# Talking-heads attention and feed-forward on one core: 42 score products a batch instead of 48, and output stores issued piece by piece

## The chip, the cores and the metric

The kernel runs on one core of a Trainium2 chip. A core has five engines with a queue each: PE (TensorE, matrix products; its weight loads are listed as PEld), DVE (VectorE), ACT (ScalarE), POOL (GpSimd) and SP (SyncE, which here only issues DMAs). Each works through its queue strictly in order, and they meet at semaphores. The metric is the device time of one execution in microseconds, as the median of several runs. Before the change the three runs took 646.55, 649.42 and 652.16 us.

## The reference

Inputs: q, k, v of (8 batches, 12 heads, 448 rows, 64), two 12x12 mixing matrices, and the weights of a feed-forward layer.

```python
scores = scale * np.matmul(q, k.transpose(0, 1, 3, 2))
scores = np.einsum('bhij,hg->bgij', scores, w_pre)      # mixes the heads
scores = scores - np.max(scores, axis=-1, keepdims=True)
attn = np.exp(scores)
attn = attn / (np.sum(attn, axis=-1, keepdims=True) + 1e-09)
attn = np.einsum('bhij,hg->bgij', attn, w_post)         # mixes them again
out = np.matmul(attn, v)
# heads side by side: x is (3584, 768)
h = np.maximum(x @ w_in, 0.0)                           # (3584, 2048)
return (h * h @ w_out)                                  # (3584, 768)
```

## The kernel before, in words

**Scores.** A matrix product takes a stationary operand of up to 128x128 and streams 448 columns past it. For a pair of heads, `kt` holds both heads' turned k, 64 partitions each (128x448). `qz` holds q turned, with zeros in the other head's 64 partitions, so that a product over all 128 partitions gives one head (L381). The 448 rows of q are split into four blocks of 112 (block r holds rows 4p + r). A batch so needs 12 heads x 4 blocks = 48 score products, each 112x448. Each is evicted from PSUM to `snat` by DVE or ACT (`copy`, L251, so that its records stand at L253 and L255). Two `snat` buffers take turns, one block each.

**Chunks.** Mixing heads needs the heads on partitions. A *chunk* is ten rows of q times twelve heads, 120 partitions. SP moves it from `snat` to a buffer `sch` by one DMA of 120 runs of 448 (a *relayout*, L404); seven `sch` buffers take turns. Then, per chunk: a product with `wmix` mixes the heads (L434), DVE finds the extreme of each row (L439), ACT takes the exponent and its sum (L442), DVE the reciprocal (L448), POOL scales the second mixing matrix by it (L451), four products turn, normalise and mix in one step (L458), and DVE or ACT evicts to `atb` (again L253, L255). A batch has 45 chunks: eleven from each block, and one of eight rows put together from the two rows left over in each block (`schl`, L407). Chunk c of batch b has the number n = 45b + c. After 22 chunks, and after the last, the products with v follow (L503).

**Turning q and k.** In the first two batches TensorE turns them (L301). From the third on, DVE or ACT packs a pair of heads (`pair_k`, `pair_q`) and SP issues two DMA transposes, k at L350 and q at L356. `kt` and `qz` have seven slots for six pairs, so a slot comes free only once the last block of an earlier pair has been scored.

**Feed-forward.** Two batches make 896 rows of x, in four units of 128 or 256 rows. A unit is products with w_in (L547), relu on ACT (L560), squaring on POOL (L563), products with w_out (L579), eviction on DVE (L594), and stores on SP (L622, L629). Since the rows lie in chunk order, a tile of 128 rows is stored in one to five DMAs.

**Order.** All of it is written down ahead of time by a planner (L55). Each operation has an engine or a choice of two, an assumed cost, a due time counted in chunks, and what it depends on. The planner runs through time, gives each free engine the ready operation with the earliest due time, and so fixes the order on every engine. Feed-forward work and stores are due last (FILL, L260) and fill gaps. A relayout is due five chunks ahead of its mix and assumed to take 0.77 us of SP and to land 4.5 us after some 0.4 us more; a DMA transpose takes 1.25 us of SP and lands 6 us later; the stores of one tile are one operation of 1.5 us, however many DMAs they are. On the chip only the order remains, and the semaphores.

Of the kernel before, what the change touches and what calls it, by code (L numbers as in the profile page):

```python
# [10 lines left out]
BF16 = mybir.dt.bfloat16  # L11
# [3 lines left out]
DMODEL = H * D  # L15
# [8 lines left out]
NR = 4  # L24
PR = S // NR
CI = 10
CPR = 11
NP = CI * CPR
KC = CI * H
NCHUNK = NR * CPR + 1  # L30
XA = 2 * NP
# [8 lines left out]
MOST = {"m": 3, "a": 2, "f": 2, "g": 4, "mix": 6}  # L40
UNITS = [(0, 128), (128, 384), (384, 640), (640, 896)]
# [103 lines left out]
def kernel(  # L145
# [20 lines left out]
    qs = sb.tile([PR, H, NR, D], BF16, name="qs")  # L166
    ks = sb.tile([P, H, NB, D], BF16, name="ks")
    vs = sb.tile([P, H, NB, D], BF16, name="vs")
    qz = many(NSLOT, "qz", [P, 2, S], BF16)
    kt = many(NSLOT, "kt", [P, NB * 128], BF16)  # L170
    qn = many(2, "qn", [PR, 2, NR * 128 + 64], BF16)
    kn = many(2, "kn", [P, NB, 2, D], BF16)
    snat = many(2, "snat", [PR, H, S], BF16)
# [16 lines left out]
    def load_q(b, h0, h1, r0=0, r1=NR):  # L190
        nc.gpsimd.dma_start(
            out=qs[:, h0:h1, r0:r1, :].rearrange("p h r d -> p h (r d)"),
            in_=q[b, h0:h1].rearrange("h (p r) d -> p h (r d)", r=NR)[:, :, r0 * D:r1 * D],
        )
# [14 lines left out]
    ident = sb.tile([P, P], BF16, name="ident")  # L209
    for h0 in range(0, H, 4):  # L210
        load_lo(ks, k, 0, h0, h0 + 4)
        load_hi(ks, k, 0, h0, h0 + 4)
        load_q(0, h0, h0 + 4, 0, 1)
        if h0 == 0:
            masks.make_identity(nc, ident[:, :])
    load_q(0, 0, H, 1, NR)
# [6 lines left out]
    for t_ in es:  # L223
# [10 lines left out]
    wmix = sb.tile([KC, P], BF16, name="wmix")  # L234
    nc.vector.memset(wmix[:, KC:P], 0.0)
    wback = sb.tile([KC, H, CI], F32, name="wback")
    nmask = sb.tile([KC, CI], F32, name="nmask")
    nc.gpsimd.tensor_scalar(
        out=nmask[:, :], in0=smask[:, :], scalar1=-SCALE, scalar2=1.0, op0=ALU.mult, op1=ALU.mult,
    )  # L240
    nc.gpsimd.tensor_tensor(
        out=wmix[:, 0:KC].rearrange("p (s h) -> p s h", s=CI),
        in0=wpre_rep[:, :].unsqueeze(1).to_broadcast([KC, CI, H]),
        in1=nmask[:, :].unsqueeze(2).to_broadcast([KC, CI, H]), op=ALU.mult,
    )
    nc.gpsimd.tensor_tensor(
# [39 lines left out]
    def t_qk(b, p):  # L286
# [4 lines left out]
        if i >= NSLOT:  # L291
            old = [score_ops[(i - NSLOT) // NPAIR, NR - 1, 2 * ((i - NSLOT) % NPAIR) + x] for x in range(2)]

        def turn(tag, at, ins, src, n, blocks, dve, act, put):
            key = (tag, "t", b, p, n, blocks[0])

            def mms(slot):
                v_ = slot[:, :].bitcast(BF16)
                for u, r in enumerate(blocks):
                    for x in range(2):  # L300
                        nc.tensor.transpose(  # L301
                            v_[64 * x:64 * x + 64, u * n:(u + 1) * n], src[:, 2 * p + x, r, :], ident[0:n, 0:n],
                        )

            mm = add("PE", 200 + 55 * len(blocks), at, keep(key, mms), ins + old, lat=200, bank=key)
# [6 lines left out]
        def put_q(c0, n):  # L312
            def go(eng, v_):
                for x in range(2):
                    copy(eng, z[64 * x:64 * x + 64, x, c0:c0 + n], v_[64 * x:64 * x + 64, 0:n])
            return go

        first = b == 0
        mk, ek = turn("g", pri, [k_in[b, p // 2]], ks, 128, range(NB), 310, 440, put_k)
        if first:  # L320
            mq, eq = turn("f", pri, [q_in[0, p // 2]], qs, PR, range(1), 300, 520, put_q(0, PR))
            ml, el = turn("g", p - 5, [q_late], qs, PR, range(1, NR), 620, 740, put_q(PR, S - PR))
            ready[b, p] = [[ek, eq]] + [[ek, el]] * 3
            got_op[b, p] = [mk, mq, ml]
        else:
            mq, eq = turn("g", pri, [q_in[b, p // 2]], qs, PR, range(NR), 780, 880, put_q(0, S))
            ready[b, p] = [[ek, eq]] * NR
            got_op[b, p] = [mk, mq]

    ready, got_op = {}, {}  # L330
# [411 lines left out]
```

## Time and profile before

| | |
|---|---|
| runs | 646.55, 649.42, 652.16 us, median 649.42 |
| profiled execution | 649.58 us, span 647.8, mean granted TensorE clock 0.975 |
| TensorE busy | 592.0 us (91%) |
| DVE busy | 509.0 us (79%) |
| ACT busy | 501.9 us (77%) |
| POOL busy | 305.3 us (47%) |
| score products (L381) | 384, 119.4 us busy |
| score evictions | 191 on DVE at 0.614 us, 193 on ACT at 0.544 us |
| relayouts | 352 of 120 runs (0.785 us to issue) and 32 small ones (0.690) |
| DMA transposes | 36 of k (1.217 us to issue) and 36 of q (1.249) |
| stores | 107 (98 at L629, 0.662 us to issue, 9 at L622, 0.461) |

The span runs from the first to the last instruction in the profile; the profiled execution's own time is 1.8 us longer. Busy is the time in which at least one record of the engine runs. In the lists, an entry in square brackets says how long the engine stood idle before the instruction and what ended that wait. SP's DMA issues are not counted as busy, but they stand in the list in order of time with their length. The granted clock is that of TensorE, as a share of full speed.

### The profile page before, as it was taken

The numbers are of one execution on the slowest core, as the hardware profiler recorded it, in microseconds if no ns is written. First come the engines' busy times: TensorE is split into PE (matmuls) and PEld (weight loads), VectorE is DVE, ScalarE is ACT, GpSimd is POOL, SyncE is SP. The second block draws the span as 40 slices with busy tenths as digits, with TensorE's granted clock in tenths as the row PEclk, the third lists the DMA queues.
The fourth block names the chain that finished last, engine by engine and source line by source line (L and its number), as shares of the span: only waits on it lengthen the run. The fifth ranks groups of instructions, "written<-read, shape, count | busy, mean of one in ns | idle before, by whom it ended". The sixth has DMA issues, their size and how long they took to land.

```text
span 647.8 us, 16877 instructions
## 1 busy us (share of the span) xinstructions
PE 592.0 (91%) x5576; PEld 425.1 (66%) x5576; DVE 509.0 (79%) x1274; ACT 501.9 (77%) x1280; POOL 305.3 (47%) x559
## 2 busy tenths in 40 slices
PE   5679799997989999997999989998899989999996
PEld 3347467765667667765767757876666757777874
DVE  7788998995789978984798879997788787988411
ACT  4698799995889878985888868998788868887420
POOL 7245528434635236623556426733464534453531
PEclk9778999998999999999999999999899999999999
DMA  9999949754697549957398567976397845623011
GB/s 106 190 201 185 204 93 192 151 120 117 109 187 141 124 137 167 158 118 117 103 183 141 129 126 143 193 147 118 113 156 155 128 117 131 150 63 109 17 50 49
DMA packets 152500, 86.44 MB, mean 133 GB/s; under 512 B 73757, under 2 KB 148957, under 8 KB 152413
## 3 DMA queue, kind: packets, MB, share of 16 engines
q1 hardware_dynamic: 104253, 62.56, 41.7%
q0 software_dynamic: 48160, 22.81, 27.7%
q8 instruction: 43, 0.70, 0.5%
q14 instruction: 44, 0.36, 0.2%
HBM read 45.62 MB, written 11.01 MB: 87 GB/s over the span
## 4 chain that ended last, share of the span: by engine, by line
PE 62%; DMA 18%; DVE 9%; issue 3%; ACT 3%; POOL 2%; SPq 1%; DVEq 0%; ACTq 0%; POOLq 0%
PE bank L547 16%; PE bank L579 16%; DMA sch<-snat 13%; PE bank L458 9%; PE bank L381 8%; PE bank L434 7%; PE bank L503 6%; DMA qz<-qn 4%; DVE mn L439 3%; ACT es L442 2%; DVE atb L253 2%; DVE snat L253 2%; DMA kt<-kn 2%; POOL wq L451 1%; SPq L404 1%
## 5 line engine op out<-in xcount | busy, mean ns | idle before, releaser
L442 ACT ACTIVATE es<-bank,mn 120x448 bf16<-120x448 f32 x360 | 229.8, 644 | 48.9 <-DVE mn L439 40.3
L451 POOL TENSOR_SCALAR wq<-wback,rc 120x120 bf16<-120x120 f32 x360 | 131.8, 370 | 248.0 <-DVE rc L448 152.5
L439 DVE TENSOR_REDUCE mn<-bank 120x1 f32<-120x448 f32 x360 | 213.8, 613 | 21.0 <-PE bank L434 20.1
L579 PE MATMUL bank<-w,h 128*128 128x384 bf16 x896 | 172.5, 325 | 0.3 <-DVE snat L253 0.3
L547 PE MATMUL bank<-xt,w 128*128 128x256 bf16 (+1 forms) x1536 | 167.3, 262 | 0.0
L253 DVE CAST atb<-bank 128x480 bf16<-128x480 f32 (+1 forms) x214 | 134.4, 637 | 33.3 <-PE bank L458 32.0
L563 POOL TENSOR_TENSOR h<-hr 128x512 bf16<-128x512 f32 x112 | 116.5, 1040 | 72.9 <-ACT hr L560 68.9
L547 PEld LDWEIGHTS <-w 128*128 128x128 bf16 x1536 | 135.0, 98 | 22.3 <-issue 0.8
L434 PE MATMUL bank<-sch,wmix 120*128 120x448 bf16 x352 | 122.0, 365 | 22.3 <-DMA sch<-snat 19.9
L458 PEld LDWEIGHTS <-es 120*128 120x128 bf16 (+1 forms) x1440 | 103.5, 99 | 56.6 <-issue 20.9
L458 PE MATMUL bank<-wq,es 120*128 120x120 bf16 (+1 forms) x1440 | 129.3, 219 | 11.4 <-POOL wq L451 10.2
L253 DVE CAST snat<-bank 112x448 bf16<-112x448 f32 x191 | 114.0, 614 | 18.4 <-PE bank L381 11.9
L381 PE MATMUL bank<-kt,qz 128*112 128x448 bf16 x384 | 119.4, 369 | 8.0 <-DMA qz<-qn 4.1
L579 PEld LDWEIGHTS <-h 128*128 128x128 bf16 x896 | 85.2, 97 | 56.2 <-issue 2.3
L255 ACT CAST snat<-bank 112x448 bf16<-112x448 f32 x193 | 98.4, 544 | 21.6 <-PE bank L381 17.6
L255 ACT CAST atb<-bank 128x480 bf16<-128x480 f32 (+1 forms) x154 | 85.2, 563 | 12.9 <-PE bank L458 11.8
L560 ACT ACTIVATE hr<-bank 128x512 f32<-128x512 f32 x112 | 67.2, 600 | 34.0 <-PE bank L547 32.2
L442 ACT ACTIVATION_READ_ACCUMULATOR es<-bank,mn 120x1 f32 x360 | 75.3, 209 | 0.0
L448 DVE RECIPROCAL rc<-sm 120x1 f32<-120x1 f32 x360 | 54.3, 154 | 21.0 <-ACT es L442 19.2
L381 PEld LDWEIGHTS <-qz 128*112 128x112 bf16 x384 | 48.8, 135 | 24.8 <-DMA qz<-qn 5.5
L434 PEld LDWEIGHTS <-wmix 120*128 120x128 bf16 x360 | 34.8, 100 | 41.4 <-DMA sch<-snat 32.5
L594 DVE COPY osb<-bank 128x384 f32<-128x384 f32 x56 | 30.9, 552 | 34.2 <-PE bank L579 28.0
(41 smaller groups left out, 243.7 us busy)
## 6 DMA issues: line engine op xcount, KB each, us to landing
sch<-snat SPq DMA_DIRECT2D x352, 105.0 KB
qs<-in_q_dram POOLq DMA_DIRECT2D x14, 336.0 KB, 13.5
vs<-in_v_dram POOLq DMA_DIRECT2D x8, 384.0 KB, 7.9
w<-in_moe_w_in_dram POOLq DMA_DIRECT2D x6, 512.0 KB, 11.1
w<-in_moe_w_out_dram POOLq DMA_DIRECT2D x4, 768.0 KB, 15.1
ks<-in_k_dram POOLq DMA_DIRECT2D x14, 192.0 KB, 14.4
out_dram<-osb SPq DMA_DIRECT2D x7, 330.0 KB
vs<-in_v_dram POOLq DMA_DIRECT2D x8, 288.0 KB, 9.6
```

What stands on the lines that cost most here:

```text
L253: nc.vector.tensor_copy(out=out_, in_=in_)
L255: nc.scalar.copy(out=out_, in_=in_)
L381: nc.tensor.matmul(slot[0:PR, 0:S], lhsT=qz[i][:, x, r * PR:(r + 1) * PR], rhs=kt[i][:, 0:S], start=True, stop=True,)
L434: nc.tensor.matmul(slot[:, 0:S], lhsT=wmix[0:rows, :], rhs=src[0:rows, :], start=True, stop=True,)
L439: nc.vector.tensor_reduce(out=mn[i][0:rows, :], in_=slots[mk][0:rows, 0:S], axis=AX.X, op=ALU.min)
L442: nc.scalar.activation(out=es[i][0:rows, 0:S], in_=slots[mk][0:rows, 0:S], func=ACT.Exp, scale=-1.0, bias=mn[i][0:rows, 0:1], accum_out=sm ...
L451: nc.gpsimd.tensor_scalar(out=wq[i][0:rows, :, 0:ns], in0=wback[0:rows, :, 0:ns], scalar1=rc[i][0:rows, 0:1], scalar2=1.0, op0=ALU.mult, o ...
L458: nc.tensor.matmul(slot[:, jb * H * ns:(jb + 1) * H * ns], lhsT=es[i][0:rows, jb * 128:(jb + 1) * 128], rhs=wq[i][0:rows, :, 0:ns], start= ...
L547: nc.tensor.matmul(slot[:, j * w:(j + 1) * w], lhsT=w1[c2][:, (f0 + j) * 128:(f0 + j + 1) * 128], rhs=xt[:, c2, a:z], start=(c2 == 0), sto ...
L560: nc.scalar.activation(out=hr[gi % 2][:, :], in_=slots[key][:, :], func=ACT.Relu)
L563: nc.gpsimd.tensor_tensor(out=h2_[:, f0:f0 + nf, 0:w], in0=hr[gi % 2][:, :].rearrange("p (f c) -> p f c", f=nf), in1=hr[gi % 2][:, :].rear ...
L579: nc.tensor.matmul(slot[:, 0:384], lhsT=h2_[:, ft, mt * 128:(mt + 1) * 128], rhs=w2[:, ft, nt * 384:(nt + 1) * 384], start=(ft == 0), stop ...
```

## The change

The 448 rows of q become three blocks of 128 rows (row 3p + j of the first 384) and a tail of 64 rows for every head. The tails of a pair of heads share one product: `load_tail` reads them into `qt`, row t of head x on partition 2t + x and in that head's 64 columns, with zeros in the others. Turned as a whole (`t_tail` on TensorE in the first two batches, `x_tail` by one DMA transpose a batch after that) it is `zt`, and its product with `kt` gives 64 rows of both heads on 128 partitions. So a batch has 6 + 3 x 12 = 42 score products, each 128x448.

The tail comes first (r = 0) and needs no `qz`. It gives six chunks; its last four rows go, two each, to the thirteenth chunks of blocks 1 and 2, which have eight rows left over; block 3's last chunk has the other eight rows of the 45 chunks' 448. First chunks of the four blocks: 0, 6, 19, 32. As the tails' partitions are ordered by head parity, their mix uses `wmix[0]`, with its rows permuted by one product with `perm` at the start; thirteenth chunks use `wmix[2]`, permuted in part. Buffers `snat` still take turns: block 1 and block 3 share one, the tail and block 2 the other.

In the first batch k and the tails are loaded ahead of the rest of q. The scaling of `wmix` moves from POOL to DVE.

`pieces` replaces `store`: each DMA of a tile's store is an operation of its own, of 0.45 us up to ten rows and 0.85 us above.

The diff, cut:

```diff
-NR = 4
-PR = S // NR
+NJ = 3
 CI = 10
-CPR = 11
-NP = CI * CPR
+CPR = 12
+NS = 64
+TAIL = S - NS
 KC = CI * H
-NCHUNK = NR * CPR + 1
-XA = 2 * NP
+C0 = [0, 6, 19, 32]
+NCHUNK = 45
+XA = 22 * CI
 XB = S - XA
 NB = 4
 W2B = 2 * S
...
+SEGS = [(0, 0, 60, TAIL)]
+for j_ in range(NJ):
+    SEGS.append((2, 60 + 130 * j_, 120, j_))
+    SEGS.append((1, 180 + 130 * j_, 8, j_))
+    if j_ < NJ - 1:
+        SEGS.append((0, 188 + 130 * j_, 2, TAIL + 60 + 2 * j_))
...
-    qs = sb.tile([PR, H, NR, D], BF16, name="qs")
+    qs = sb.tile([P, H, NJ, D], BF16, name="qs")
+    qt = sb.tile([P, NPAIR, P], BF16, name="qt")
+    zt = sb.tile([P, NPAIR, P], BF16, name="zt")
...
-    qz = many(NSLOT, "qz", [P, 2, S], BF16)
+    qz = many(NSLOT, "qz", [P, 2, NJ * P], BF16)
...
-    snat = many(2, "snat", [PR, H, S], BF16)
+    snat = many(2, "snat", [P, H, S], BF16)
...
+    for t_ in wmix[1:]:
+        nc.vector.tensor_tensor(
...
+        def put_q(eng, v_):
+            for x in range(2):
+                copy(eng, z[64 * x:64 * x + 64, x, :], v_[64 * x:64 * x + 64, 0:NJ * P])
+
+        mk, ek = turn("g", pri, [k_in[b, p // 2]], ks, NB, 310, 440, put_k)
+        at = p - 5 if b == 0 else pri + 3
+        mq, eq = turn("g", at, [q_in[b, p // 2]], qs, NJ, 700, 800, put_q)
+        ready[b, p] = [[ek]] + [[ek, eq]] * NJ
+        got_op[b, p] = [mk, mq]
...
+        pri = b * NCHUNK - 19 + 3 * g
+        mm = add("PE", 200, pri, keep(key, mms), [tail_in[b]] + old, lat=200, bank=key)
+        ev = add({"DVE": 360, "ACT": 440}, 0, pri, put, [mm], frees=key)
...
+    def x_tail(b):
+        old = [score_ops[b - 1, 0, p] for p in range(NPAIR)]
+
+        def turn():
+            nc.sync.dma_start(
+                out=zt[:, :, :], in_=qt[:, :, :].rearrange("p a c -> p (a c)"), transpose=True,
+            )
+
+        pri = b * NCHUNK - 22
+        op = add("SP", 1250, pri, turn, [tail_in[b]] + old)
+        done = add("TURN", 800, pri, lambda: None, [op], lat=6000)
+        got_tail[b] = [done]
+        for p in range(NPAIR):
+            ready_tail[b, p] = done
+
...
-        ready[b, p] = [[tk_op[i], tq_op[i]]] * NR
+        ready[b, p] = [[tk_op[i]]] + [[tk_op[i], tq_op[i]]] * NJ
...
     def score(b, r, h):
-        p, x = divmod(h, 2)
+        p, x = (h, 0) if r == 0 else divmod(h, 2)
...
-        sn = snat[(b * NR + r) % 2]
-        tag = "mfag"[h % 4] if b == 0 and r == 0 else "g"
+        sn = snat[(b * (NJ + 1) + r) % 2]
...
         def mms(slot):
-            nc.tensor.matmul(
-                slot[0:PR, 0:S], lhsT=qz[i][:, x, r * PR:(r + 1) * PR], rhs=kt[i][:, 0:S], start=True, stop=True,
-            )
+            w = zt[:, p, :] if r == 0 else qz[i][:, x, (r - 1) * P:r * P]
+            nc.tensor.matmul(slot[:, 0:S], lhsT=w, rhs=kt[i][:, 0:S], start=True, stop=True)
 
         def evac(eng):
-            copy(eng, sn[:, h, :], slots[key][0:PR, 0:S])
-
-        pri = b * NCHUNK + CPR * r - AHEAD - 9 + 0.7 * h
-        n = b * NR + r - 2
+            copy(eng, sn[:, h, :], slots[key][:, 0:S])
+
+        nh = NPAIR if r == 0 else H
+        pri = b * NCHUNK + C0[r] - AHEAD - 0.6 - 0.7 * (nh - h)
+        n = b * (NJ + 1) + r - 2
         old = list(relay_of[n]) if n >= 0 else []
-        mm = add("PE", 190, pri, keep(key, mms), ready[b, p][r] + old, lat=200, bank=key)
...
+        sn = snat[(b * (NJ + 1) + r) % 2]
+        lat = 5500 if b == 0 and c else 4500
+        here = relay_of.setdefault(b * (NJ + 1) + r, [])
+        deps = [scopy[b, r, h] for h in range(NPAIR if r == 0 else H)]
+        pri = n - AHEAD
+        if r > 0 and cc == CPR and r < NJ:
+            src_of[n] = schl[r - 1]
+            here.append(move(n, pri, 700, deps + side.get((b - 1, r), []), schl[r - 1][0:96, :], sn[120:P, :, :], lat))
+            return
+        src_of[n] = sch[len(ring) % NSCH]
+        old = [m_op[ring[-NSCH]]] if len(ring) >= NSCH else []
+        ring.append(n)
+        if r == 0:
+            srcs, rows = sn[2 * CI * cc:2 * CI * (cc + 1), 0:NPAIR, :], KC
+        elif cc == CPR:
+            srcs, rows = sn[120:P, :, :], 96
+        else:
+            srcs, rows = sn[cc:cc + CPR * (CI - 1) + 1:CPR, :, :], KC
+        here.append(move(n, pri, 770, deps + old, src_of[n][0:rows, :], srcs, lat))
+        if r == 0 and cc == 5:
+            for j in range(1, NJ):
+                here.append(move(
+                    b * NCHUNK + C0[j + 1] - 1, pri + 0.5, 500, deps + side.get((b - 1, j), []),
+                    schl[j - 1][96:KC, :], sn[116 + 4 * j:120 + 4 * j, 0:NPAIR, :], lat,
+                ))
...
+        wm = wmix[0 if r == 0 else 2 if cc == CPR else 1]
...
+        half = 0 if c < 22 else 1
+        m = m_op[n] = add("PE", 190, n, keep(mk, f_m), relay[n] + [at_op.get(n - NE), w_ready], lat=200, bank=mk)
...
-                if z == W2B and mt == 1 and pair == B // 2 - 1:
-                    add("SP", 1500, FILL, lambda si=si, mt=mt, nt=nt: store(pair, a + mt * 128, osb[si % 2], nt), [ev])
...
-            ix_store[0] += 1
-            sp = add("SP", 1500, FILL, lambda si=si, mt=mt: store(pair, a + mt * 128, osb[si % 2]), [ev0, ev])
-            st_op[si] = add("DMA", 800, FILL, lambda: None, [sp], lat=2500)
+                whole = not (z == W2B and mt == 1 and pair == B // 2 - 1)
+                evs = evs + [ev] if nt == 1 and whole else [ev]
+                if nt == 1 or not whole:
+                    done = []
+                    for rows, dst, o in pieces(pair, a + mt * 128, None if whole else nt):
+                        def store(dst=dst, o=o, rows=rows, si=si, e0=0 if whole else nt * 384, e1=384 if not whole and nt == 0 else DMODEL):
+                            nc.sync.dma_start(out=dst, in_=osb[si % 2][o:o + rows, e0:e1])
+                        done.append(add("SP", 450 if rows <= CI else 850, FILL, store, evs))
+                    st_op[si] = add("DMA", 800, FILL, lambda: None, done, lat=2500)
...
+    def w_turn(slot):
+        nc.tensor.matmul(
+            slot[0:KC, 0:KC], lhsT=perm[:, :], rhs=wmix[1][:, 0:KC], start=True, stop=True,
+        )
...
+        if b < 2:
+            t_tail(b, 0)
+            t_tail(b, 1)
+        else:
+            x_tail(b)
...
+                    if g0 == 0:
+                        tails = [load(1e5, n, lambda b=b, x=x: load_tail(b + 1, x), got_tail[b] + gate(n)) for x in range(2)]
+                        tail_in[b + 1] = add("DMA", 0, n, lambda: None, tails, lat=0)
```

## The prediction

> **What bounds the kernel now.** I read the page first: the share of each engine, the forty slices, the chain that ended last.
>
> ```profile
> span 647.8 us, 16877 instructions
> PE 592.0 (91%) x5576; PEld 425.1 (66%) x5576; DVE 509.0 (79%) x1274; ACT 501.9 (77%) x1280; POOL 305.3 (47%) x559
> ...
> PE   5679799997989999997999989998899989999996
> ...
> PEclk9778999998999999999999999999899999999999
> ...
> PE 62%; DMA 18%; DVE 9%; issue 3%; ACT 3%; POOL 2%; SPq 1%; DVEq 0%; ACTq 0%; POOLq 0%
> ```
>
> TensorE is full except at the start, at the end and in a few dips of one or two slices. The 592 us overstate its work, since a matmul's record holds its drain: the list in order of time shows products of 448 columns starting 0.19 us apart, though each record is 0.35 us long. So one 448-column product costs 0.19 us where TensorE is full.
>
> The dips come about once in 75 us, where one batch hands over to the next. The windows, the list in order of time and the waits show what ends them:
>
> ```profile
> 296.00:300.00 4.00, 4.00 (x42) 3.43 (x39) 2.38 (x6) 3.56 (x10) 2.66 (x5) 1.00 0.77 120
> 300.00:304.00 4.00, 0.94 (x8) 0.53 (x7) 0.58 (x2) 0.82 (x2) 1.86 (x3) 1.00 1.24 105
> 304.00:308.00 4.00, 3.43 (x16) 2.00 (x16) 1.48 (x4) 1.63 (x4) 0.46 (x1) 0.59 0.78 137
> ```
> ```profile
> 303.15 0.58 PE L381 MATMUL bank<-kt,qz 128*112 128x448 bf16 x2 [3.02 <-DMA qz<-qn]
> ```
> ```profile
> 449.39 0.80 SPq L629 DMA_DIRECT2D out_dram<-osb  x1
> 450.30 1.25 SPq L356 DMA_TRANSPOSE qz<-qn  x1
> 451.64 3.71 SPq L404 DMA_DIRECT2D sch<-snat  x4
> ```
> ```profile
> 454.82 0.50 PE L434 MATMUL bank<-sch,wmix 120*128 120x448 bf16 x1 [3.43 <-DMA sch<-snat]
> ```
> ```profile
> PE bank L434 <- DMA sch<-snat: 19.9, 26, 3.4
> ```
>
> In the windows the columns after the length are the busy times of PE, PEld, DVE, ACT and POOL, then the granted clock. At 300 us TensorE stands 3.0 us for a turned q and then runs 4 us at a clock of 0.59. At 451 us a relayout is issued late, behind a store and a q turn on SP, and its mixing product comes 3.43 us late; at 154 us it is the same (3.00 us). From 80 to 600 us the 40 us windows add up to 28 us without TensorE, 16.5 us of it (40 to 600 us) in front of mixing products that wait for a relayout.
>
> **The change, part by part**, against the profiled execution (649.58 us, span 647.8, 1.8 us around it; the median of the runs, 649.42, is the same to 0.03%). The compiled order of the changed program gives the counts.
>
> *Score products:* 384 become 336. That the change does not do this is excluded, the order has 336. 48 x 0.19 = 9.1 us of TensorE. In the first two batches, where TensorE turns q, 96 transposes become 72 and 13 come in (12 of tails, one for the mixing matrix): 11 fewer, at 24 in 0.78 us (16.65 us) 0.4 us. Beside full TensorE both count: **-9.5**. If the stretch is bound otherwise the gain there is nothing: bounds 0 and -9.5; I take all, because in 240 to 280 us TensorE lacks only 0.55 of 40 us.
>
> *Evictions:* 48 fewer, at 0.614 us on DVE and 0.544 us on ACT: 27.8 us, 14 on each. That those of 128 partitions take as long as those of 112 I take from the eviction of 128x456, 0.546 us on ACT. The copies of q (`pair_q`, L343) shrink from 512 to 384 columns: 36 x a quarter of 0.28 to 0.64 us, 4 us in all. This lies beside TensorE, save where the chain runs through evictions; it gives them 2% (DVE snat) and not much more on ACT, some 16 us, an eighth of which goes: **-2** (bounds 0 and -16, the 14 and 2 of each engine, were these the limit).
>
> *q off the first block:* tails need k and zt; q is needed only by block 1. The answer on tile qz:
>
> ```profile
> its engine sat idle before it (us, times) until:
>   DMA qz<-qn: 9.6, 9
> ```
>
> zt is turned at 24 to 29 chunks ahead of its batch, some 40 us, so it is no wait. But the last turn of k is issued 2 to 5 chunks ahead, and the last product of the first block stands 2 to 5 chunks ahead of the batch (3 to 5 before): one SP issue earlier than the last q, no more. So I take half of the 9.6, the clock's dips with it: **-5**. Bounds 0 and -14 (9.6, and 4.3 for the three slow stretches: 5 us at 0.70, 4 at 0.71, 4 at 0.59).
>
> *SP:* relayouts 384 -> 376 (8 more large, 16 fewer small: 8 x 0.79 - 16 x 0.69 = -4.7), six turns of qt at 1.25 (+7.5; a narrower q turn costs what a k turn does, 1.22 to 1.25), stores 107 -> 126 (79 small instead of 47 at 0.46, 47 large instead of 60 at 0.82: +4.1). Sum +6.9 us in 648, about 1 us a batch on a queue that issues about 61 us a batch (44 x 0.79, 4 x 0.69, 12 x 1.25, 13.4 stores of 0.63) of 75. Against that, a store of several pieces was planned as one piece of 1.5 us whatever its length (four took 2.66 us at 307.92), and each piece now has its own place and a cost near the measured one: a relayout is held up by one piece, at most 0.86 us. Behind each turn and piece on SP stand relayouts, and behind those the mixing product. **0**, bounds -8 (half of the 16.5) and +7.
>
> *The new wait:* block 1's twelve products can only be planned once block 3 of the batch before has left its buffer (both are snat1), and all stand within two chunks, 8 to 6 chunks ahead of the first mix that needs them. The planner assumes 4.5 us for a relayout's landing; the first one here landed after 6.5 us (15.88 to 22.41). Their evictions wait for it at the head of DVE and ACT, with the minima, exponents and atb copies behind them, and TensorE's next mixes behind those. Nearest row: evictions waiting for sch, 3.9 us in 7 and 2.2 in 2, 0.7 us each. Seven batches at 0.7: **+5**. Bounds 0 and 7 x 3.4 (the longest wait for a relayout) = +24.
>
> *Start and end:* the first relayout needs 6 evictions and no q copies instead of 12 and 12 (3 to 3.5 us less on each of two engines), but DVE's prelude grows by a 0.38 us memset and four or five small operations of about 0.25 us, and block 1, needed six chunks later instead of eleven, still waits for the same q loads. **-1**, bounds -3 and +2. The last store goes from three issues to two, 0.4 us, inside that. POOL has 14 more load issues at 0.7 to 0.8 us beside 47% busy: 0. The tails' loads have the 64-element runs of the first q loads (3.8 us to land) and come in the previous batch: 0.
>
> Sum: -9.5 - 2 - 5 + 0 + 5 - 1 = -12.5: 649.6 becomes **637**.
>
> [...]
>
> **The rivals.**
>
> *Slower: the turnover of block 1 stalls.* The burst of twelve evictions meets a late relayout in each of seven batches; DVE and ACT stand, block 1's first relayouts are issued late on an SP that is already full there (125.99 to 155 us shows it issuing without a pause), and TensorE runs out of filler. Price: 7 x (3.4 us of wait + 1.5 us at the low clock, the mean of the three dips' 4.3) = 34, less 9.5 + 2 + 1: +21, **671**; it decides from about 2 us a batch lost (14 of the 17.5 that the other terms gain). For it: the dips of today are of this kind, on the same queue. Against: the last products of a block stood 6 chunks ahead of use before too, and evictions waited little. [...]
>
> *No change: the gain is eaten.* TensorE has less work but stands for the same relayouts, and the new wait takes 7 x 1.0: -9.5 + 7 - 1 = **646**. For it: 16.5 us of idle come from relayouts, which the change does not shorten.
>
> [...]
>
> **How the numbers follow.** Forecast 637, its own range 629 to 643: 0.48. No change, around 646: 0.20. Faster still: 0.15. Slower: 0.17. The runs of before spread from 646.55 to 652.16, so 1% is about what can be told from no change; below 642.9 lies the forecast nearly whole and the fast rival: faster 0.63, within 1% 0.21, slower 0.16. The range 621 to 655 leaves out most of the slow rival and the edge of the fast one.
>
> **What would show it.** 336 score products still 0.19 us apart, and TensorE's busy time down by 9 to 15 us (0.31 us of record a product at most). Idle before score products on qz near 0. The three clock dips at the even batches gone or shorter; the wait of mixing products for sch no longer than 20 us. Evictions waiting for sch under 10 us in all: more than 20 is the slow rival. SP's busy time up by about 7 us. I am wrong if TensorE's busy time falls and its idle time grows as much, or if block 1's first mix, seven times, stands more than 2 us.

## The result and the profile after

The changed kernel takes 672.1 us (median; 668.8 to 674.9) against 648.9 of the kernel before on the same chips: ratio **1.035**, 95% interval 1.028 to 1.042. It is 3.5% slower where 637 us, 1.9% faster, was forecast. The profiled execution took 671.08 us. Of `mem_own_pe`, below, three runs of ten took 654 to 659 us and are not counted.

First the page of the changed kernel:

```profile
span 669.1 us, 16736 instructions
PE 595.3 (89%) x5517; PEld 419.3 (63%) x5517; DVE 501.3 (75%) x1258; ACT 488.9 (73%) x1241; POOL 313.9 (47%) x572
...
PE   5768799986879989798889998989997998999997
...
PEclk9668799998999999799989998999999998999999
...
PE 64%; DMA 20%; DVE 8%; issue 3%; SPq 2%; POOL 1%; ACT 1%; DVEq 0%; ACTq 0%; POOLq 0%
```

TensorE's busy time has not fallen (592.0 before), and there are more dips than before, in the middle of batches too. The waits of TensorE and of SP's queue (engine, line, what it waited for: us in total, times, longest) say for what:

```profile
PE bank L504 <- DMA sch<-snat: 35.9, 28, 5.0
...
PE bank L436 <- DVE snat L277: 6.3, 4, 3.1
PE bank L436 <- DMA kt<-kn: 4.9, 6, 1.6
```
```profile
SPq L372 <- DMA qt<-in_q_dram: 26.0, 6, 6.7
```

L504 is now the mixing product, L436 the score product, L372 the turn of the tails. No score product waits for a turned q on its way (`DMA qz<-qn`) any more; the wait of mixing products for relayouts rose from 19.9 to 35.9 us; and SP, which issues every relayout, stands 26.0 us in front of six turns until the tails have landed. The third such turn, in the lists in order of time of POOL, SP and TensorE:

```profile
253.90 0.90 POOL L200 DMA_DIRECT2D qs<-in_q_dram  x1
254.80 0.67 POOL L211 DMA_DIRECT2D ks<-in_k_dram  x1
255.45 0.68 POOL L217 DMA_DIRECT2D ks<-in_k_dram  x1
256.10 1.37 POOL L206 DMA_DIRECT2D qt<-in_q_dram  x2
```
```profile
261.45 0.62 SPq L665 DMA_DIRECT2D out_dram<-osb  x1
267.72 1.26 SPq L372 DMA_TRANSPOSE zt<-qt  x1
269.08 6.68 SPq L459 DMA_DIRECT2D sch<-snat  x7
```
```profile
275.95 0.56 PE L504 MATMUL bank<-sch,wmix 120*128 120x448 bf16 x1 [4.96 <-DMA sch<-snat]
```
```profile
264.00:272.00 8.00, 7.00 (x68) 5.55 (x66) 7.21 (x19) 6.96 (x20) 6.76 (x11) 1.00 1.34 167
272.00:280.00 8.00, 4.05 (x15) 2.18 (x16) 2.47 (x5) 2.60 (x7) 2.36 (x5) 0.65 0.97 198
```

The tails' load is issued behind one of q and two of k. SP issues nothing from 262.1 to 267.7. Seven relayouts follow at 269, too late: TensorE stands 4.96 us, and the clock is 0.65 in the window of 272 to 280. The DMA packets in the trace show a second delay behind the first. Packets of SP's queue that start in each us (a relayout moves packets of 896 bytes, the turn of 256):

```
us from the start    267  268  269  270  271  272  273  274  275
relayouts (896 B)     39    7    0    0    0    0   24  113  103
the turn (256 B)       0    0  273   65   93  324   13    0    0
```

This turn's own transfer takes 4.15 us beside the loads, and until it is through no packet of a relayout starts.

Where the 21.3 us of span come from can be read from the spans. *Idle* is the span less TensorE's busy time. *Clock* is (1 - mean clock) x span: what the lowered clock adds to the busy time, a little too much, since part of it is idle. Busy less clock is TensorE's work at full clock. In the changed kernel products of 448 columns start 0.37 us apart at a clock of 0.5 and 0.19 at 1.0 (medians of L504 and L436). Each row is one profiled execution; that of `pe_lumped` was the shortest of its kernel's runs, those of `pe_turn` and `before_minus48_order` the longest of theirs.

| profiled execution | span | idle | clock | work |
|---|---|---|---|---|
| before | 647.8 | 55.8 | 16.2 | 575.8 |
| after | 669.1 | 73.8 | 32.1 | 563.2 |
| `turn_late` | 649.7 | 64.1 | 23.4 | 562.2 |
| `pe_tail` | 647.8 | 60.8 | 24.0 | 563.0 |
| `pe_wait` | 655.1 | 68.1 | 24.9 | 562.1 |
| `pe_turn` | 666.4 | 72.4 | 34.7 | 559.3 |
| `pe_lumped` | 640.9 | 56.0 | 22.4 | 562.5 |
| `before_minus48_order` | 654.3 | 67.1 | 20.3 | 566.9 |

The work fell by 12.6 us, somewhat more than the 9.5 forecast; idle rose by 18.0 and the clock's part by 15.9.

### The profile page after: what moved, and what is told of

Read it like the earlier page. It is cut to its first block, busy times and chain, and to the rows that moved or that the text cites. A ratio compares the mean times of both kernels' runs of the same rounds, so it can differ in the third digit from the quotient of the medians.

```text
span 669.1 us, 16736 instructions
## 1 busy us (share of the span) xinstructions
PE 595.3 (89%) x5517; PEld 419.3 (63%) x5517; DVE 501.3 (75%) x1258; ACT 488.9 (73%) x1241; POOL 313.9 (47%) x572
## 4 chain that ended last, share of the span: by engine, by line
PE 64%; DMA 20%; DVE 8%; issue 3%; SPq 2%; POOL 1%; ACT 1%; DVEq 0%; ACTq 0%; POOLq 0%
PE bank L641 18%; PE bank L609 16%; DMA sch<-snat 14%; PE bank L528 8%; PE bank L504 8%; PE bank L436 7%; PE bank L565 6%; DVE mn L509 3%; DMA kt<-kn 2%; DVE atb L277 2%; DMA qt<-in_q_dram 2%; DVE snat L277 1%; DMA schl<-snat 1%; SPq L459 1%; DVE rc L518 1%
## 5 line engine op out<-in xcount | busy, mean ns | idle before, releaser
L521 POOL TENSOR_SCALAR wq<-wback,rc 120x120 bf16<-120x120 f32 x360 | 130.1, 366 | 254.2 <-DVE rc L518 149.8
L509 DVE TENSOR_REDUCE mn<-bank 120x1 f32<-120x448 f32 x360 | 213.8, 613 | 23.4 <-PE bank L504 22.2
L277 DVE CAST atb<-bank 128x480 bf16<-128x480 f32 (+1 forms) x224 | 143.7, 650 | 54.6 <-PE bank L528 52.2
L641 PE MATMUL bank<-w,h 128*128 128x384 bf16 x896 | 176.7, 330 | 0.7 <-DVE snat L277 0.4
L504 PE MATMUL bank<-sch,wmix 120*128 120x448 bf16 (+1 forms) x344 | 120.4, 370 | 38.2 <-DMA sch<-snat 35.9
L609 PEld LDWEIGHTS <-w 128*128 128x128 bf16 x1536 | 137.2, 100 | 24.5 <-issue 0.4
L279 ACT CAST snat<-bank 128x448 bf16<-128x448 f32 x175 | 89.0, 544 | 34.7 <-PE bank L436 28.2
L277 DVE CAST snat<-bank 128x448 bf16<-128x448 f32 x161 | 96.2, 615 | 22.1 <-PE bank L436 11.7
L436 PE MATMUL bank<-kt,qz 128*128 128x448 bf16 x288 | 89.1, 374 | 7.6 <-DVE snat L277 6.3
L279 ACT CAST atb<-bank 128x480 bf16<-128x480 f32 (+1 forms) x136 | 77.5, 573 | 18.9 <-PE bank L528 18.1
L504 PEld LDWEIGHTS <-wmix 120*128 120x128 bf16 x360 | 35.1, 100 | 52.9 <-DMA sch<-snat 40.0
L436 PEld LDWEIGHTS <-qz 128*128 128x128 bf16 x288 | 28.6, 103 | 30.8 <-issue 16.2
```

What stands on the lines that cost most here:

```text
L277: nc.vector.tensor_copy(out=out_, in_=in_)
L279: nc.scalar.copy(out=out_, in_=in_)
L436: nc.tensor.matmul(slot[:, 0:S], lhsT=w, rhs=kt[i][:, 0:S], start=True, stop=True)
L504: nc.tensor.matmul(slot[:, 0:S], lhsT=wm[0:rows, :], rhs=src[0:rows, :], start=True, stop=True,)
L509: nc.vector.tensor_reduce(out=mn[i][0:rows, :], in_=slots[mk][0:rows, 0:S], axis=AX.X, op=ALU.min)
L521: nc.gpsimd.tensor_scalar(out=wq[i][0:rows, :, 0:ns], in0=wback[0:rows, :, 0:ns], scalar1=rc[i][0:rows, 0:1], scalar2=1.0, op0=ALU.mult, o ...
```

## The experiments

One thing holds for nearly all of them. Whenever an edit changes what the planner plans, it writes another order for PE, DVE, ACT and POOL as well: the traces show their instructions in another sequence. Only `before_minus48_order`, `before_noloads` and `pe_lumped_noloads` keep the sequence of PE, DVE and ACT of the kernel that they start from. What a new order does without any other change was measured three times: -1.5 us (`before_1400`), +8.6 us (`before_pieces`) and +8.4 us (`before_minus48` against `before_minus48_order`). So a difference of up to some 9 us between two of the other kernels is not by itself the price of the edit.

### Is it the turn of the tails?

Four kernels. `turn_late` issues the turn later:

```diff
         def turn():
+            with tc.issue_after(relay_ins[b * NCHUNK - 20].ins):
                 nc.sync.dma_start(out=zt..., in_=qt..., transpose=True)
...
-        op = add("SP", 1250, pri, turn, [tail_in[b]] + old)
+        op = add("SP", 1250, pri, turn, [tail_in[b], relay[b * NCHUNK - 20][0]] + old)
```

> The changed kernel with one difference: SyncE may issue the turn of the tails (zt) only behind the relayout that runs 20 chunks ahead of the batch, so it stands 17 to 18 chunks before its batch instead of 24 to 29; nothing else moves. Theory 1 (the queue of SyncE stands in front of this turn for the tails' load, 26.0 us in six batches, the relayouts behind it come late, and TensorE waits for them and then runs at a lower clock): the 26 us go to under 5, the mixing products' wait for relayed chunks falls from 35.9 us to 15 to 22, and the time is 650 to 658. Theory 2 (the turnover of snat before block 1, the prediction's slow rival, makes the loss): no change, 668 to 674. Theory 3 (the stores, now 450 to 850 us in pieces on the planner's account, displace relayouts): no change, 668 to 674.

`pe_tail` has no such turn:

```diff
-        if b < 2:
-            t_tail(b, 0)
-            t_tail(b, 1)
-        else:
-            x_tail(b)
+        t_tail(b, 0)
+        t_tail(b, 1)
```

> The changed kernel with the tails turned on TensorE, as in the first two batches, in all eight: six transposes and two evictions of 384 columns a batch more, one turn on SyncE and its wait less in batches 2 to 7. Theory 1: SyncE no longer waits for a load ahead of a batch; the evictions cost 6 x 0.8 = 5 us of VectorE and ScalarE and the transposes 6 x 0.4 = 2 us of TensorE; 650 to 660. Theories 2 and 3: 672 to 680, since only work is added.

`before_plus_turn` adds `load_tail` (for one pair of heads) and `x_tail`, both unused, to the kernel before.

> The kernel before, with, added and unused, a small load of tails into a tile qt (64 rows of one pair of heads, two transfers a batch) behind its loads of q and k, and one turn of this tile on SyncE in batches 2 to 7; nothing else. It prices the turn's place in SyncE's order apart from the blocks. Theory 1: SyncE stands in front of the added turn for some 20 to 30 us in all, and the kernel gets slower by 6 to 20 us: 655 to 669. Theories 2 and 3: at most the turns' own issue, 6 x 1.25 us, partly hidden: 647 to 653.

`load_first` moves the two lines that load the tails ahead of `got`, the loads of q and k.

> The changed kernel with the two loads of the tails issued ahead of the loads of q and k on GpSimd's queue, in place of behind them; the turn stays where SyncE's order has it, 28 to 31 chunks ahead. Theory 1 (SyncE waits for the tails' load, which is issued late and lands slowly): the 26 us of SyncE's wait fall below 8, and the time is 648 to 658. If the turn itself, or the count of its packets, were the price: 668 to 674.

Measured: `turn_late` **650.9** (ratio to before 1.005, 1.001 to 1.009), `pe_tail` **648.1** (0.998, 0.995 to 1.002), `before_plus_turn` **667.3** (1.029, 1.023 to 1.034), `load_first` **669.7** (1.029, 1.025 to 1.033). So the turn, at the place that it has on SP, is worth 21 to 24 us, more than an order alone did; the blocks of 128 rows without it are as fast as the kernel before, and the kernel before with such a turn, of one pair of heads, is 18 us slower. SP's wait in `before_plus_turn`:

```profile
SPq L344 <- DMA qt<-in_q_dram: 28.5, 6, 7.5
```

`turn_late` met its time but not the whole of its account. SP's wait for the tails is gone and "nothing else moves" does not hold, since the order is new; the wait of mixing products stayed above the expected 15 to 22 us. It and that of `pe_tail`:

```profile
PE bank L508 <- DMA sch<-snat: 29.2, 27, 3.2
```
```profile
PE bank L504 <- DMA sch<-snat: 23.6, 20, 3.0
```

`load_first` was a miss for the wait as the only cause:

```profile
SPq L372 <- DMA qt<-in_q_dram: 11.9, 7, 3.4
```

The wait fell from 26.0 us to this, though not below 8, and the time hardly moved. The turn then stood 28 to 31 chunks ahead, amid the loads. So wait and transfer were separated. Both kernels are `pe_tail` with one DMA a batch added on SP, 24 to 28 chunks ahead:

```diff
 # pe_wait
+            nc.sync.dma_start(out=scr[0:1, :], in_=qt[0:1, 0, 0:D])
 # pe_turn
+            with tc.issue_after(relay_ins[b * NCHUNK - 29].ins):
+                nc.sync.dma_start(out=scr[:, :, :], in_=w2[:, 0, 0:5 * P], transpose=True)
```

> The changed kernel with the tails turned on TensorE (648.1), and, added in batches 2 to 7, a copy of 128 bytes on SyncE that waits for the tails' load and stands 24 to 28 chunks ahead of the batch, where the changed kernel has its turn. It brings back the wait without the turn's transfer. If the wait in SyncE's order is the cause: SyncE waits some 25 us for the load and the time is 664 to 674. If the turn's own transfer beside the loads is the cause: 646 to 652.

> The same as the run above with the other half: in the same places of SyncE's order a turn of 128 x 640 elements that waits for no load (its source is a weight that has long landed; the result is unused). If the wait is the cause: 647 to 654, the turns' issue of 6 x 1.3 us at most. If the transfer beside the loads is the cause, as the run with the loads issued first (669.7) suggests: 662 to 674.

Measured: `pe_wait` **657.3** (1.013, 1.008 to 1.018), `pe_turn` **663.4** (1.020, 1.014 to 1.027), against 648.1 of `pe_tail`. The kernel with the wait alone is 9 us slower, that with the transfer alone 15. `pe_wait` so lies between its two expectations, `pe_turn` in that of the transfer. In `pe_wait`:

```profile
SPq L373 <- DMA qt<-in_q_dram: 24.4, 6, 7.7
```
```profile
PE bank L501 <- DMA sch<-snat: 33.2, 22, 5.8
```

and in `pe_turn`, where SP waits for no tail:

```profile
PE bank L504 <- DMA sch<-snat: 42.6, 31, 4.3
```

against the 23.6 us of `pe_tail`. In both it is mixing products that stand without their relayout, but not at the same chunks. The six turns of the changed kernel are issued in batches 1 to 6, between the twelfth and the eighteenth mix of the batch. The starts of the mixing products give the time from mix 8 to mix 20, added up over these six batches:

| | mix 8 to mix 20, six batches |
|---|---|
| before | 108.2 us |
| after | 132.4 |
| `turn_late` | 112.2 |
| `pe_tail` | 110.8 |
| `before_plus_turn` | 125.1 |
| `load_first` | 133.0 |
| `pe_wait` | 124.7 |
| `pe_turn` | 115.6 |

The changed kernel loses 24 us to the kernel before in these stretches, as much as its whole loss, and `pe_tail` loses 3. So the loss stands where the turn stands, whatever the new order does elsewhere. The wait alone is seen at work in the same way: `pe_wait` takes 14 us more than `pe_tail` here, some of which it wins back elsewhere. The transfer is not: `pe_turn` loses 5 us of its 15 here, and three of its four longest waits for a relayout (4.3, 3.1 and 2.6 us) stand at chunks 39 to 43 of a batch, over twenty chunks behind the turn. So the wait is shown; that the transfer alone costs 15 us is not, since a new order could account for the rest.

### Is it the stores in pieces?

`before_pieces` is the kernel before with the change's `pieces`; `after_lumped` and `pe_lumped` undo it in the changed kernel and in `pe_tail`:

```diff
-                    for rows, dst, o in pieces(...):
-                        def store(...): nc.sync.dma_start(...)
-                        done.append(add("SP", 450 if rows <= CI else 850, FILL, store, evs))
+                    def store(...):
+                        for rows, dst, o in pieces(...): nc.sync.dma_start(...)
+                    done = [add("SP", 1500, FILL, store, evs)]
```

> The kernel before with its stores as one operation of the plan for each piece (450 or 850 ns) in place of 1500 ns for a tile; the same DMAs. Theory 3 (piecewise stores push relayouts back): slower by 5 us or more, 654 to 665. Theories 1 and 2: within 1%, 645 to 654; the prediction had 0 for this part.

> The changed kernel with its stores planned as before, one operation of 1500 ns for all pieces of a tile; the DMAs are the same. In the kernel before, the split of this operation cost 8.6 us (657.7 against 649.1). If that price is the same in the changed kernel: 661 to 666 against 672. If it is a matter of where the planner happens to put things in the old kernel, or if the late relayouts hide it: 669 to 675.

> The changed kernel with both: the tails turned on TensorE in all batches (648.1 by itself) and the stores planned as one operation a tile. If the stores' split costs what it cost in the kernel before: 637 to 642. If it costs nothing here: 645 to 651.

`before_1400` replaces 1500 by 1400 in the kernel before.

> The kernel before with one number of the plan changed: a tile's store counts 1400 ns in place of 1500; the instructions and their DMAs are the same, only the order that the planner writes moves. It measures what such a reordering alone does to the time. If the +8.6 us of the stores in pieces was the price of the pieces: within 2 us of the kernel before, 647 to 651. If orders of the planner scatter by some us whatever the reason: any time from 643 to 660, and differences of a few us between such variants say nothing of the edit.

Measured: `before_pieces` **657.7** (1.015, 1.010 to 1.019), `after_lumped` **666.1** (1.027, 1.021 to 1.033), `pe_lumped` **645.2** (0.992, 0.989 to 0.995), `before_1400` **648.4** (0.998, 0.997 to 1.000). The pieces cost 8.6 us in the kernel before; in the changed one the medians differ by 6.0 (with intervals that overlap), in `pe_tail` by 2.9 (intervals that just overlap). The DMAs of each pair are the same, so this is the order alone; that a new order need not cost anything, `before_1400` shows. Why the finer account gives a worse order was not found out.

`pe_lumped` ran once more under the label `pe_lumped_1400` (the number in it means nothing):

> The kernel with the tails turned on TensorE and one planned store a tile (645.2) once more, on another chip and in five rounds, beside the three above. If its gain is real: 642 to 648 and an interval below 1.

It took **643.9** (0.993, 0.990 to 0.996). Tails on TensorE and one planned store a tile make the change a version that is 0.7 to 0.8% faster than the kernel before. Whether these 4 to 5 us come from the blocks of 128 rows or from this version's order is not shown.

### Is it the new wait of block 1?

`mem_own_pe` gives the tails' products a buffer of their own, in space that `mem_pe` frees too:

```diff
-        sn = snat[(b * (NJ + 1) + r) % 2]
+        sn = stail if r == 0 else snat[(b * NJ + r - 1) % 2]
```

> A control for the next: the changed kernel with the tails turned on TensorE, and with space freed in SBUF: six buffers of qz in place of eight, hr and wback in bf16, the permutation kept in a tile of weights that is overwritten later. hr in bf16 halves what the hidden layer's eviction writes and what its following step on GpSimd reads, which may gain some us; six buffers of qz bind the turn of q to the batch before. Within 1% of 648: 642 to 654 by all theories.

> The control with, in the freed space, a buffer of its own for the products of the tails, so that blocks 1 to 3 alternate over the two snat buffers and block 1 no longer waits for the relayouts of the last block of the batch before; its products stand 19 to 7 chunks ahead and no longer in a burst 8 to 6 chunks ahead. Theory 2 in its small form (the prediction's +5 for this turnover): 4 to 10 us below the control, 638 to 644 if the control is at 648. Theory 2 in its large form (the slow rival, 34 us): 20 us or more below it. If the turnover costs nothing: within 2 us of the control.

Measured: `mem_pe` **647.9** (0.999, 0.996 to 1.001) and `mem_own_pe` **651.0** (1.001, 0.997 to 1.005; seven runs from 643 to 652). Taking the wait away gains nothing that can be seen. In `mem_pe` score products wait 7.8 us for evictions or relayouts; in `mem_own_pe` these waits are gone, but the mixing products' wait rose from 22.1 to 30.2 us. The two versions also differ in their order, and a gain of a few us may hide behind that. The large form, 20 us or more, is excluded.

### Where does the gain on the products stay?

Two kernels leave 48 products and their evictions out of the kernel before; in `before_minus48` `score` returns early for the odd heads of block 3, in `before_minus48_order` the planner still plans them:

```diff
         def mms(slot):
+            if r == NR - 1 and h % 2:
+                return
...
         def evac(eng):
+            if r < NR - 1 or h % 2 == 0:
                 copy(eng, sn[:, h, :], slots[key][0:PR, 0:S])
```

> The kernel before with 48 score products and their 48 evictions left out (the odd heads of the fourth block of each batch are not computed; the old values are relayed in their place), nothing else changed. It prices the saving of the change apart from all that the change adds. If a product pays its 0.19 us of TensorE, as in the prediction: 9 us and, with the evictions' bounds, up to 16 less, 633 to 641. If the products fill time that TensorE would spend waiting or at a lower clock: 645 to 650.

> The kernel before without the 48 products and 48 evictions of the odd heads of the fourth block, as in the earlier run (661.2), but the planner still plans them, so that every other instruction stays in the order of the kernel before. If the earlier run was slow because the planner wrote another order: 636 to 644 here, the products' 9 to 12 us being gained. If less work on TensorE only lets it run into the relayouts earlier and stand there, whatever the order: 646 to 664.

Measured: **661.2** (1.019, 1.016 to 1.022) and **652.8** (1.006, 1.003 to 1.009). Leaving work out made the kernel slower, by 11 us with a new order and by 4 us in the old one. The old order's waits of TensorE:

```profile
PE bank L437 <- DMA sch<-snat: 24.6, 26, 2.6
...
PE bank L383 <- DMA qz<-qn: 5.1, 4, 3.3
```

against 19.9 and 4.1 before. In the table above its work is 8.9 us less than before, its idle time 11.3 more, its clock's part 4.1 more, in an execution that is 3 us above the median. The work left out came back as idle time and a lower clock. Of the idle time, 4.7 us more stands in front of mixing products and 1.0 in front of products that wait for q; that TensorE, with less to do, only reaches the relayouts earlier is the likely reading, but these rows carry half of it at most.

Three kernels leave out loads, to see whether this happens in the loads' bursts. `pe_lumped_noload` drops the tails' loads from the second batch on, from the plan too (`tails = []`); in the other two `lambda: load_q(...)` becomes `lambda: b < 1 and load_q(...)`, and so for k, v and the tails, and the planner still plans them:

> The changed kernel with the tails turned on TensorE and the stores planned as one operation a tile (645.2), and, from the second batch on, without the loads of the tails (the first batch's tails are used again): 7 x 2 transfers of 384 packets of 128 bytes fewer. If these packets cost time beside the other transfers: 638 to 643. If not: 643 to 648.

> The kernel before without its 48 loads of q, k and v for the third to the eighth batch (old values are used again); every other instruction stays in its order. With the next run it tells whether the loads' burst, in which relayouts land late, is what holds the kernel back. If it does: 625 to 640. If the loads cost nothing: 646 to 651.

> The repaired version of the change (tails turned on TensorE, one planned store a tile; 644 to 645) without the loads of q, k, v and the tails for the third to the eighth batch. If the gain on the products, 9 to 12 us of TensorE's work, is eaten in the loads' bursts alone: 8 to 12 us below the run above. If it is eaten by waits and a lowered clock anywhere, the bursts or not: the same 4 to 6 us below it as with the loads.

Measured: `pe_lumped_noload` **642.0** (0.989, 0.986 to 0.993), `before_noloads` **639.5** (0.984, 0.982 to 0.987), `pe_lumped_noloads` **636.5** (0.981, 0.978 to 0.983). The loads cost 10 us in the kernel before and 7 to 9 in the repaired change. Without the tails' loads it is 2 to 3 us faster, in a new order, so that this is not shown to be the price of their packets. Without loads the repaired change is ahead of the kernel before by 3.0 us, with them by 4 to 5. So the 9 to 13 us of work are not lost in the bursts; most of them turn into waits and low clock elsewhere too. That it is the pace of the relayouts which decides there is an argument: what a faster pace would give was not tried.

## Why the prediction was wrong

**The turn of the tails: this step failed.** The prediction wrote "zt is turned at 24 to 29 chunks ahead of its batch, some 40 us, so it is no wait", "the tails' loads ... come in the previous batch: 0" and, for SP, six turns of 1.25 us of issue. All three ask whether the *user* of zt waits, and it never does. None asks what stands in SP's queue *behind* the turn, an operation that waits for a load that POOL issues last: the next relayouts, which are issued 7.2 us (median) ahead of their mixes. SP's issue time, the sum of its DMA issues' lengths, was forecast well (468.1 to 478.2 us, +10 where +7 was said); the 26.0 us of waiting and the six transfers, 2.1 to 5.8 us each, were not in the term, which was 0 with +7 as its upper bound. The runs give 24 us for it (672.1 less 648.1), the whole of the loss of 23, and the stretch from mix 8 to mix 20 gives the same 24. How much of it is the wait and how much the transfer stays open: with the wait alone a kernel is 9 us slower, with a small turn and the wait 18, and the 15 us of the transfer alone lie for the most part elsewhere.

**The order.** The section on the kernel before says that the planner "fixes the order on every engine". That is wrong for SP: the set handed to `manual_schedule` at the kernel's end names PE, DVE, ACT and POOL. SP's own order is left to the framework, and the turn stands in it 24 to 29 chunks ahead where the planner's due time is 22. "Each piece now has its own place" on SP therefore did not follow from the planner's costs: the pieces changed what the planner believed of SP, and through that the order of the other four, which is another one in the trace of `before_pieces`. The term was part of the same 0; it measured +3 to +9.

**Score products, -9.5.** The count and the size are right: 336 products, work down by 12.6 us. What failed is taking all of it off the time "because in 240 to 280 us TensorE lacks only 0.55 of 40". One full window stood for a span with 55.8 us of idle time, and the lower bound of 0 that the prediction itself named was the better value: in the kernel before, in its own order, leaving out 48 products made the time 0.6% longer.

**Evictions, -2.** DVE and ACT lost 7.7 and 13.0 us of busy time, 20.7 in all. Neither is the bound; no run shows a gain from it.

**q off the first block, -5.** The wait for turned q is gone, as said. In its place score products wait 4.9 us for kt ("the last turn of k is issued 2 to 5 chunks ahead") and 6.3 us for evictions. So no gain is left of it, and none shows in any version.

**The new wait, +5.** No run shows it: `mem_own_pe` has it not and is not faster. Evictions waited for relayouts once, 4.6 us on DVE, where over 20 us was the mark of the slow rival.

**The slow rival** gave 671 us and the kernel took 672. That was luck: as the cause of the loss its mechanism is refuted. Taking block 1's turnover away did not help, taking the turn away gave all back, and the four waits of over 1 us behind a turn (2.7, 5.0, 1.1 and 4.4 us) stand at chunks 15 to 17 of a batch, not at its end, where that turnover is. The waits at the end of a batch are no worse than before (1.1 to 2.9 us at chunks 40 to 43 after, 1.0 to 3.4 before). A time that fits is no evidence for the mechanism behind it.

**The fast rival** did not come either: no score product waits for a turned q any more and the stores are planned piece by piece, but the clock's part of the span grew from 16.2 to 32.1 us.

**Start, -1.** The first mix came at 21.26 us instead of 22.41. Not foreseen was the handover from the first batch to the second: at the sixteenth mix of batch 1 the changed kernel is 3.8 us behind the kernel before and `pe_tail` 5.6, with a clock of 0.83 and 0.84 in place of 1.00 in the window of 60 to 80 us. Its cause was not tested.

**The marks for being wrong.** The first, TensorE's busy time falling while idle grows as much, came in a harsher form: work fell by 12.6 us and idle grew by 18.0, but the lowered clock stretched the records (a score product's from 0.35 us at 1.0 to 0.58 at 0.5), so that busy time did not fall at all (592.0 to 595.3 us, where 9 to 15 less was forecast). The second, block 1's first mix standing more than 2 us, did not come: that mix waits for nothing in any of the eight batches.

## What to carry to other kernels

When a DMA that waits for something is put into a queue that others share, ask first what stands behind it in that queue, and only then whether its user waits. Ask the same of its transfer: at the third turn no packet of a relayout started for 4.15 us, until the turn was through, though what that costs alone was not settled here. Time saved on the busiest engine counts only where that engine's work, and not a chain that feeds it, sets the pace: take the engine's idle time over the whole span as the measure, and leave the work out once, in the same order, to see what it is worth. A planner's costs steer only the queues that it is given, and any change to them can rewrite the order of all the others: compare the time of the stretch in which the edit acts, and not the total alone.

## What the runs showed of the hardware

*A wait of 2.03 us was followed by a lower clock, one of 2.04 us was not.* In `pe_tail` one wait of 2.03 us, with no other beside it, stands ahead of a stretch at half the clock:

```profile
384.46 0.35 PE L504 MATMUL bank<-sch,wmix 120*128 120x448 bf16 x1 [2.03 <-DMA sch<-snat]
```
```profile
380.00:382.00 2.00, 2.00 (x37) 1.91 (x35) 0.99 (x4) 2.00 (x7) 0.78 (x3) 1.00 0.43 84
382.00:384.00 2.00, 0.43 (x6) 0.18 (x4) 1.25 (x3) 0.72 (x3) 2.00 (x3) 1.00 0.64 211
384.00:386.00 2.00, 1.54 (x10) 0.86 (x10) 0.00 (x0) 0.57 (x1) 0.29 (x1) 0.75 0.51 96
386.00:388.00 2.00, 2.00 (x22) 2.00 (x20) 1.15 (x2) 1.19 (x3) 0.00 (x0) 0.50 0.59 182
388.00:390.00 2.00, 2.00 (x18) 1.35 (x17) 1.21 (x5) 1.74 (x5) 0.65 (x1) 0.90 0.46 135
```

The clock (the eighth figure, after POOL's) is 0.50 in the window of 386 to 388, with TensorE full before and after the wait. A wait of 2.04 us in the changed kernel is followed by no such stretch; its clock stays at 1.00 until 346 us:

```profile
322.40 0.36 PE L504 MATMUL bank<-sch,wmix 120*128 120x448 bf16 x1 [2.04 <-DMA sch<-snat]
```

The clock records tell the two apart. In the traces of the kernels before and after, every change between 1.0 and 0.5 falls on a grid of 3.413 us in each, to within 2 ns. Taking the windows of that grid from 100 us on, up to the last with a whole one behind it, by TensorE's busy share in them: of the 311 at full clock ten are busy for 1% to 40%, and each is followed by a window at 0.5; of the 301 others, the lowest busy for 47% and 48%, none is. Of the windows at 0.5 the ten that are busy for 83% or more are followed by full clock, and the two that are busy for 54% and 78% by another at 0.5. So there half the clock, for 3.4 us or longer, followed each time where TensorE stood for 2.06 us or more in all within one window (60% of 3.413), and never where it stood for 1.80 us or less. The wait of 2.04 us is cut by the window's end at 322.1, and the window ahead of that end is busy for 47%. In `pe_tail` the half clock begins at 385.0, by the share of 0.75 from 384 to 386, and lasts to 388.4, 3.4 us; a window that ends there begins at 381.6, and the wait of 2.03 us, from 382.43 on, lies whole in it. The changed kernel has twelve stretches at 0.5, of 3.4 to 10.2 us, 65.9 us in all, the kernel before six, 34.5 us.

*A turn alone and beside loads.* With no load under way packets of 256 bytes, those of turns, started at 966 a us, 247 GB/s (`pe_wait`, at 271 us; 825 a us in the kernel before, at 276), and relayouts reached 261 packets of 896 bytes a us, 234 GB/s (changed kernel, at 278 us). Beside the loads the turn's 768 packets took 2.1 to 5.8 us in the changed kernel, and 0 to 41 relayout packets a us started meanwhile, where `pe_tail` has 66 to 85 a us on average in its six bursts of loads from 105 to 497 us, and the kernel before 72 to 83. Part of this lack is the wait ahead of the turn, in which SP issued no relayout: in `pe_turn`, where relayouts are issued up to the turn, 32 to 80 a us start beside it.
